# Memory-augmented attention in 64 sequential segments: the order of all engines in a block of four segments written down whole, in place of planned times and rules

## The chip, the cores and the metric

The kernel runs on one core of one Trainium2 chip, in one launch. The metric is the device time of that core in microseconds (us), the median of several runs. TensorE is called PE, VectorE DVE, ScalarE ACT, GpSimd POOL and SyncE SP, as in the profile.

## The reference

Phase 1 is attention over 64 segments of 32 tokens, in which each segment also sees 8 rows of memory: the first 8 output rows of the segment before. Phase 2 is a layer norm and a two-layer MLP. The sequence has 2048 tokens, width 512, 32 heads of 128 (`Wq`, `Wk`, `Wv`: 512 x 32 x 128), and 1792 hidden units.

```python
mem = mem0
for s in range(n_seg):                                   # 64, one after the other
    xs = x[:, s * seg_len:(s + 1) * seg_len, :].copy()
    h = jnp.concatenate([mem, xs], axis=1)               # 8 + 32 rows
    q = jnp.einsum('btd,dhe->bhte', h, Wq)
    k = jnp.einsum('btd,dhe->bhte', h, Wk)
    v = jnp.einsum('btd,dhe->bhte', h, Wv)
    scores = jnp.einsum('bhqe,bhke->bhqk', q, k) * scale
    scores = jnp.where(mask[None, None], scores, -1000000000.0)
    p = _softmax(scores, axis=-1)
    o = jnp.einsum('bhqk,bhke->bhqe', p, v)
    o = jnp.einsum('bhte,hed->btd', o, Wo)
    mem = o[:, :M, :].copy()                             # the next segment needs it
    outs.append(o[:, M:, :])
...
h = x + _A_ref(_layernorm(x, axis=-1), ...)
h2 = h + _B_ref(_layernorm(h, axis=-1), ...)             # layer norm, W1, gelu, W2
```

## The kernel before, in words

All weights lie in SBUF. A segment can't start its projections until the memory rows of the one before are there, so the segments form one long chain, and PE is kept busy in its waits with work that doesn't hang on the memory. Four segments make a block of 128 tokens; a segment's place in its block, its number modulo 4, is called its kind (0 to 3; `sg` in the code).

A segment, in the order of PE, with the names of the tiles:

1. Q and K projections of the 24 + 8 rows that depend on this segment (`hT`; the 8 are the memory rows, put there last by the two additions `hT<-TT`): Q0, Q1, K0, K1, 16 groups of four matmuls with 512 columns, each four in 32-column tiles. `passes` (L858) issues them; L873 is a matmul with its weight load, L606 one that keeps the weights that are there. ACT copies a bank to `kq`, DVE transposes it (`KALL` for K, `QT` for Q; L914), POOL copies Q into `ZC`, which holds it in block form.
2. The scores of the memory rows' queries, in two halves of 16 heads: SC0 and SC1 (`sc_mm`, L1042, `quad<-KALL,ZC`). Between and behind them lie V0 and V1 (`ps<-WV,hT`), the V projections. SC1 needs the transposed K1.
3. Softmax of each half (`sc_softmax`): DVE takes the row maximum of two parts (`nmc`, L1050), ACT the exponentials of each part (`EC`), DVE a reciprocal for each part (`rsc`, L1064) and the scaled product for each part (`PC`, L1067), then one transpose (`PTC`, L1069). The names of the plan are nmc0, ra0, PCa0, rsc0, PC0, PTC0 for the first half (the "a" ones are the first part), and the same with 1 for the second.
4. PV0 and PV1 (`pv_c`, L1080 and L1085): probabilities times V, in 64-row tiles. Between them lie PVA (L1148), the other rows' output of the segment before from the block-diagonal `BD`, and the first WO matmuls. ACT or DVE copies the outputs to `OT` (OTm0, OTm1 for the memory rows, OTx0, OTx1 for the others), the last half of V to `VS` (VS0, VS1, VSl1).
5. WO (L1176, 64 matmuls), its result transposed by DVE (`TT`, L1188), and the two additions to `hT` (L1182), with which the next segment starts. The other rows' additions go to `opT` (opA in the plan).
6. SA (`sa_mm`, L1110): the scores of the other rows, whose softmax runs into the next segment: `nma`, `SA`, `sma`, `rsa` on DVE and ACT, then `PA` on POOL (L1131), `PTA` on DVE (L1133), and four copies `BD` on POOL (L1137).

What doesn't depend on the memory is called F: K, Q and V of the rows that a whole block shares (`hB`, in kinds 0, 1 and 2) and WO for the block before (kind 3), eight groups a segment, spread between the steps above to fill the waits. Its result is folded by seven POOL operations for each half (L1228 to L1232: `TTS`, `TTB`, `opT`), in the segments behind. The layer norm of a later block (`xr`, `agg`, `rst`, `xn`, then copies to `hB` and `hT`) and the residual and statistics of an earlier one are placed there too.

The order on each engine is set by a list scheduler in the kernel (`Sched.schedule`, L237). `ORDERS` gives PE's order for each kind outright. For the other engines each operation has a duration, a fixed hop to its users (`HOP`), and, where `PLAN` has its name, a planned time in the segment; the scheduler takes operations by those times and puts each in the earliest free place of its engine, or of the cheaper of two. For the work that is not in the plan (folds, layer norm, copies of `hB`) rules hand it out behind given operations (`held`, `late`, `now`, `turned`, `fold`, in `tail`).

```python
PLAN = {"kq2": (1.72,) * 4,                              # L43
...
        "rsc0": (5.1,) * 4,
...
        "nmc1": (5.19,) * 4,
...
        "BD": (15.41,) * 4,
...
STEP = 10.28                                             # L102
```

So nearly every name has one time for all four kinds, counted from the segment's first matmul; 10.28 is the step of the plan, the length of a segment in it. `align` (L478) counts PE's instructions and puts up to 8 extra weight loads ("pads") ahead of matmuls, so that a segment of each kind starts at a set place in a fetch block of 256 instructions (`PHASE` (0, 64, 128, 192)).

Of the kernel before, what the change touches and what calls it, by code (L numbers as in the profile page):

```python
# [1694 lines left out]
```

## Time and profile before

| what | us |
|---|---|
| median of 3 runs | 806.22 (805.17, 806.22, 806.32) |
| span of the profiled execution | 804.0 |
| opening: weights arrive, segment 0 | 0 to 51.96 |
| segments 1 to 62 | 51.96 to 689.49: 637.5, 10.28 each |
| segment 63 and phase 2 | 689.49 to 804.0 |

The span of the profile is 2.2 us shorter than the median of the runs; the profile has one time of its own, its span. Times in the text below are microseconds from the span's start, or, where it says "into the segment", from the segment's first Q or K matmul. A row of a timeline has its start, its length, engine, line, operation, tiles (out<-in), shapes, and in brackets the idle time of the engine before it with what ended it.

### The profile page before, as it was taken

What the parts mean: (1) busy time and instruction counts of PE and PEld (TensorE: products, weight loads), DVE (VectorE), ACT (ScalarE), POOL (GpSimd) and SP (SyncE); (2) the same over time, 40 slices, a digit from 0 to 9 for tenths busy, and PEclk for the clock granted to TensorE, in tenths of its full rate; (3) what the DMA queues carried; (4) which work ended last, traced back from release to release, by engine and by line L of the source; (5) the groups of instructions that cost most, each with busy time, mean ns of one, the idle gap of its engine ahead of it and who ended that gap; (6) DMA issues with size and microseconds to landing.
All of it is one profiled execution on the core that took longest, in us unless ns stands there. A gap on an engine that the chain in (4) does not pass through costs nothing.

```text
span 804.0 us, 43669 instructions
## 1 busy us (share of the span) xinstructions
PE 772.7 (96%) x19317; PEld 419.3 (52%) x18821; DVE 616.6 (77%) x1975; ACT 543.0 (68%) x1618; POOL 350.7 (44%) x886
## 2 busy tenths in 40 slices
PE   3788999999999999999999999999999999999998
PEld 1345555555555555555555555555555555544443
DVE  3267898898989898998989898989898887824211
ACT  2456777777777777777777787777777777743342
POOL 5023334545454545454545454545463535367200
PEclk9999999999999999999999999999999999999999
DMA  9960010110101010101010102020212131264200
GB/s 338 393 188 16 4 30 11 27 34 23 37 18 42 18 43 14 46 10 47 8 50 10 49 11 51 10 51 3 51 29 63 37 87 32 89 167 132 69 27 26
DMA packets 65450, 48.04 MB, mean 60 GB/s; under 512 B 29028, under 2 KB 61676, under 8 KB 65260
## 3 DMA queue, kind: packets, MB, share of 16 engines
q1 hardware_dynamic: 64928, 44.98, 18.9%
q8 instruction: 150, 2.46, 1.3%
q14 instruction: 40, 0.33, 0.1%
q10 hardware_dynamic: 332, 0.27, 0.1%
HBM read 31.08 MB, written 8.13 MB: 49 GB/s over the span
## 4 chain that ended last, share of the span: by engine, by line
PE 91%; DVE 3%; DMA 2%; SPq 2%; ACT 1%; issue 0%
PE ps L873 43%; PE ps L1176 16%; PE ps L606 7%; PE quad L1584 6%; PE ps L1577 5%; PE ps L1215 4%; PE quad L1080 3%; DMA WQ<-in_A_Wq_dram 2%; SPq L776 2%; PE ps L1110 2%; PE quad L1042 2%; PE ps L1370 2%; PE quad L1148 1%; PE quad L1085 1%; DVE PC L1067 1%; ACT kq L891 1%
## 5 line engine op out<-in xcount | busy, mean ns | idle before, releaser
L873 PE MATMUL ps<-WQ,hT 128*32 128x512 bf16 x2048 | 157.0, 382 | 3.5 <-DVE hT L1182 3.3
L1176 PE MATMUL ps<-WO,OT 128*32 128x256 bf16 x4224 | 141.5, 275 | 1.0 <-ACT OT L891 1.0
L873 PE MATMUL ps<-WV,hT 128*32 128x512 bf16 x1780 | 138.1, 379 | 0.0
L892 ACT ACTIVATE kq<-ps 128x512 bf16<-128x512 f32 x146 | 87.2, 597 | 57.5 <-PE ps L873 57.2
L1131 POOL TENSOR_TENSOR PA<-SA,rsa 128x256 bf16<-128x256 f32 x64 | 39.8, 622 | 181.4 <-DVE rsa L1124 169.6
L891 ACT CAST kq<-ps 128x512 bf16<-128x512 f32 x160 | 93.3, 583 | 29.8 <-PE ps L873 29.8
L1176 PEld LDWEIGHTS ps<-WO,OT 128*32 128x32 bf16 x4224 | 96.2, 96 | 23.6 <-ACT OT L891 4.0
L1137 POOL COPY BD<-PTA 32x192 bf16<-32x192 bf16 x256 | 95.7, 374 | 16.5 <-DVE PTA L1133 0.8
L1067 DVE SCALAR_TENSOR_TENSOR PC<-EC,rsc,even 128x128 bf16<-128x128 f32 x256 | 94.5, 370 | 6.7
L873 PE MATMUL ps<-WK,hT 128*32 128x512 bf16 x1292 | 92.3, 379 | 0.0
L873 PEld LDWEIGHTS ps<-WQ,hT 128*32 128x32 bf16 x2048 | 56.4, 96 | 63.7 <-issue 19.3
L914 DVE STREAM_TRANSPOSE KALL<-kq 128x256 f32<-128x256 f32 x160 | 70.5, 441 | 21.3 <-ACT kq L891 19.0
L891 ACT CAST VS<-ps 128x512 bf16<-128x512 f32 x189 | 83.9, 444 | 0.9
L1059 ACT ACTIVATE EC<-quad,nmc 128x64 f32<-128x64 f32 x252 | 76.8, 310 | 5.7
L606 PE MATMUL ps<-WK,hT 128*32 128x512 bf16 x756 | 74.3, 379 | 0.0
L891 ACT CAST OT<-quad 128x128 bf16<-128x128 f32 (+1 forms) x208 | 68.4, 352 | 4.9 <-PE quad L1085 0.7
L914 DVE STREAM_TRANSPOSE QT<-kq 128x256 f32<-128x256 f32 x128 | 57.0, 446 | 16.1 <-ACT kq L892 15.0
L873 PEld LDWEIGHTS ps<-WV,hT 128*32 128x32 bf16 x1780 | 49.4, 96 | 34.9 <-issue 1.0
L1580 ACT ACTIVATE WQ<-ps,b1t 128x512 bf16<-128x512 f32 x42 | 28.9, 687 | 52.0 <-PE ps L1577 52.0
L1122 ACT ACTIVATE SA<-SA 128x256 f32<-128x256 f32 x64 | 26.7, 417 | 52.2 <-DVE SA L1121 48.8
L873 PEld LDWEIGHTS ps<-WK,hT 128*32 128x32 bf16 x1292 | 35.9, 97 | 46.6 <-issue 20.2
L1228 POOL TENSOR_TENSOR opT<-TTB,TTS 32x64 bf16<-32x64 f32 x128 | 40.3, 315 | 31.7 <-DVE opT L1182 22.5
(159 smaller groups left out, 1475.9 us busy)
## 6 DMA issues: line engine op xcount, KB each, us to landing
WV<-in_A_Wv_dram SPq DMA_DIRECT2D x4, 1024.0 KB, 10.4
WK<-in_A_Wk_dram SPq DMA_DIRECT2D x4, 1024.0 KB, 18.1
WQ<-in_A_Wq_dram SPq DMA_DIRECT2D x4, 1024.0 KB, 19.4
WO<-in_A_Wo_dram SPq DMA_DIRECT2D x16, 256.0 KB, 7.7
v_last<-VSB SPq DMA_DIRECT2D x60, 64.0 KB, 3.1
VBD<-v_last SPq DMA_DIRECT2D x60, 64.0 KB, 2.9
h_mid<-xr SPq DMA_DIRECT2D x16, 128.0 KB, 1.8
WQ<-h_mid SPq DMA_DIRECT2D x4, 512.0 KB, 4.4
```

The lines of the kernel that those rows point to most:

```text
L606: return e.add_instruction(mybir.InstMatmult(name="I-%d" % (4000000 + _kept[0]), engine=mybir.EngineType.PE, start_tensor_calc=start, stop ...
L873: ins = e.matmul(o, l, m, start=(k == 0), stop=(k == DC - 1), tile_position=(0, 32 * j), skip_group_check=True)
L891: return {"act": (lambda e: e.copy(out, src), t_act(n, ps_)), "dve": (lambda e: e.tensor_copy(out, src), 0.155 + 1.0e-3 * n * fast)}
L892: return {"act": (lambda e: e.mul(out, src, scale_), t_act(n, ps_)), "dve": (lambda e: e.tensor_scalar(out, src, scale_, None, ALU.mult), ...
L914: S.op("dve", lambda e: e.transpose(out, src), reads=[("kq", i)], writes=[key], dur=t_dve(256) + 0.02)
L1059: return e.activation(EC[:, r, sl, :], o[:, sl, :], ACTF.Exp, bias=nmc[:, r, sl:sl + 1], accum_out=smc[:, r, sl:sl + 1])
L1067: S.op("dve", lambda e, sl=sl, xc=xc: e.scalar_tensor_tensor(PC[:, r, :, :, sl], xc, rsc[:, r, sl:sl + 1], ev, ALU.mult, ALU.mult), reads= ...
L1137: S.narrow(S.op("pool", lambda e, j=j, rows=rows: e.tensor_copy(BD[rows, par, :, j, :, :], PTA[rows, :, 0:NA, :]), reads=["PTA"], writes=[ ...
L1176: ins = e.matmul(ps[bank][32 * j:32 * j + 32, 0:256], lhs(slot(h)), wo_cols(h, b), start=(k == 0), stop=(k == 15), tile_position=(0, 32 * ...
L1228: return e.tensor_tensor(o[32 * q:32 * q + 32, c:c + 2], x, y, ALU.add)
L1577: ins = e.matmul(ps[bank][:, 0:SBT], W1[:, cc, fc * P:(fc + 1) * P], hnT_of(k)[:, cc, :], start=(cc == 0), stop=(cc == DC - 1))
L1584: S.op("pe", lambda e: e.matmul(quad[:, t, :], gT_of(k, fc)[:, t * P:(t + 1) * P], W2[:, fc, :], start=(fc == 0), stop=(fc == FC - 1)), re ...
```

## The change

The plan has a time for each operation in each of the four segments of a block, now also for the folds (f0a to f13), the layer norm (lnst, ag, rs, xn, hB, hTx), the residual (xadd, st2a and so on) and each of the four BD copies. These times are no longer wishes: all planned operations of an engine are sorted by them and chained, one after the other, so the order on an engine is the table's. The engine of each operation is in a table of its own (`HOME`, by name and kind), its duration too (`DUR`). The step of the table is 10.181. The rules for folds and the rest are gone.

```diff
-PLAN = {"kq2": (1.72,) * 4,
...
-        "rsc0": (5.1,) * 4,
...
-        "nmc1": (5.19,) * 4,
...
-STEP = 10.28
...
+PLAN = {'kq2': (1.735, 1.758, 1.443, 1.553),
...
+        'rsc0': (5.374, 5.143, 5.398, 5.014),
...
+        'nmc1': (5.16, 5.218, 5.184, 5.194),
...
+        ('ZCm0', 2): 'act',
...
+        ('PCa0', 3): 'pool',
...
+        ('OTx0', 3): 'dve',
+        ('OTx1', 3): 'dve',
...
+STEP = 10.181
+PHASE = 32
...
+        rows = {e: [] for e in ENGINES}
+        for o in self.rec:
+            at = planned(o)
+            if at is not None and not o.is_dma:
+                o.eng = HOME.get((o.kind, o.tag[0] % 4), o.eng)
+                if o.alts:
+                    o.fn, o.dur = o.alts[o.eng]
+                o.dur = DUR.get((o.kind, o.eng), o.dur)
+                rows[o.eng].append((STEP * o.tag[0] + at, o.gidx, o))
+        for row in rows.values():
+            row.sort()
+            for a, b in zip(row, row[1:]):
+                b[2].order = a[2]
+                a[2].succ.append(b[2])
...
-                    t = max(t, q.start + q.dur + (SWITCH if q.mode != o.mode else 0.0))
+                    t = max(t, q.start + q.dur + (SWITCH if q.mode != o.mode and (o.tag is None or o.tag[0] == 0) else 0.0))
...
-            if PHASE and o.tag is not None and o.tag[0] != seg:
-                seg = o.tag[0]
-                owed = (LATE.get(seg, PHASE[seg % 4]) - at) % FETCH_N
+            if o.tag is not None and o.tag[0] // 4 > seg:
+                seg = o.tag[0] // 4
+                owed = (PHASE - at) % FETCH_N
...
+                def halves(e, sl=sl):
+                    return [e.tensor_scalar(PC[:, r, b, :, sl], EC[:, r, sl, :], rsc[:, r, sl:sl + 1], even[:, b:b + 1], ALU.mult, ALU.mult) for b in range(2)][1]
+                S.either({"dve": (whole, 0.37), "pool": (halves, 0.85)}, reads=[ek, rk, "even"], writes=[pk])
...
-            after = [S.last_writer.get(("hTm", (s + 1) % RING))] if s + 1 < NS else []
```

Smaller parts: two operations of one engine that only read the same PSUM bank no longer wait for each other; the pads come once a block; `PA` no longer waits for the next segment's `hT`; hops and durations of some PE operations differ in the planner; the PE orders (`ORDERS`) are new for all kinds. A split of K1 in two (`k_split`) is in the code and used nowhere.

What this does to the streams, at three places. The lines of the changed kernel are other lines of the same operations (L1288 is SC, L1105 and L843 are the projections, L1332 is PV, L1296 nmc, L1311 rsc, L1316 PC, L1321 PTC, L1146 the transposes of `kq`, L1384 PTA).

PE in a segment of kind 0, from SC0 to PV0, before:

```order
L1042 MATMUL quad<-KALL,ZC 32x64 x16
L873 MATMUL ps<-WV,hT 32x512 x4
L606 MATMUL ps<-WV,hT 32x512 x4
L873 MATMUL ps<-WV,hT 32x512 x12
L873 MATMUL ps<-WK,hB 32x512 x4
L1042 MATMUL quad<-KALL,ZC 32x64 x16
L873 MATMUL ps<-WV,hT 32x512 x4
L873 MATMUL ps<-WK,hB 32x512 x4
L873 MATMUL ps<-WV,hT 32x512 x8
L873 MATMUL ps<-WK,hB 32x512 x4
L1080 MATMUL quad<-PTC,VS 128x2x16 x8
```

and now:

```order
L1288 MATMUL quad<-KALL,ZC 32x64 x16
L1105 MATMUL ps<-WV,hT 32x512 x16
L843 MATMUL ps<-WV,hT 32x512 x4
L1288 MATMUL quad<-KALL,ZC 32x64 x16
L1105 MATMUL ps<-WV,hT 32x512 x8
L1105 MATMUL ps<-WK,hB 32x512 x8
L1105 MATMUL ps<-WV,hT 32x512 x4
L1105 MATMUL ps<-WK,hB 32x512 x4
L1332 MATMUL quad<-PTC,VS 128x2x16 x8
```

The second SC, SC1, stood behind six groups after SC0 and now stands behind five; five groups lay between it and PV0, now six. The other three kinds show the same shift, with Q or V of the shared rows, or the last block's WO, in place of `WK,hB`. In kind 1 the last eight matmuls before PV0 are `WV,hT`.

DVE in a segment of kind 0, the softmax of both halves, before:

```order
L1064 RECIPROCAL rsc<-smc 128x1
L1067 SCALAR_TENSOR_TENSOR PC<-EC,rsc,even 128x128
L1064 RECIPROCAL rsc<-smc 128x1
L1050 TENSOR_REDUCE nmc<-quad 128x2
L1067 SCALAR_TENSOR_TENSOR PC<-EC,rsc,even 128x128
L1069 STREAM_TRANSPOSE PTC<-PC 128x128
L1064 RECIPROCAL rsc<-smc 128x1
L1067 SCALAR_TENSOR_TENSOR PC<-EC,rsc,even 128x128
L1064 RECIPROCAL rsc<-smc 128x1
L1067 SCALAR_TENSOR_TENSOR PC<-EC,rsc,even 128x128
L1069 STREAM_TRANSPOSE PTC<-PC 128x128
```

and now:

```order
L1311 RECIPROCAL rsc<-smc 128x1
L1316 SCALAR_TENSOR_TENSOR PC<-EC,rsc,even 128x128
L1296 TENSOR_REDUCE nmc<-quad 128x2
L1311 RECIPROCAL rsc<-smc 128x1
L1316 SCALAR_TENSOR_TENSOR PC<-EC,rsc,even 128x128
L1321 STREAM_TRANSPOSE PTC<-PC 128x128
L1311 RECIPROCAL rsc<-smc 128x1 x2
L1316 SCALAR_TENSOR_TENSOR PC<-EC,rsc,even 128x128 x2
L1321 STREAM_TRANSPOSE PTC<-PC 128x128
```

The row maximum of SC1 (`nmc`) has moved ahead of the first half's second reciprocal (rsc0), in kinds 0 and 2; in kinds 1 and 3 it stays behind it. In kind 3 one `PC` of the first half goes to POOL.

DVE from the transpose of K0 to that of K1, in a segment of kind 1, before:

```order
L914 STREAM_TRANSPOSE KALL<-kq 128x256
L1133 STREAM_TRANSPOSE PTA<-PA 128x128
L914 STREAM_TRANSPOSE QT<-kq 128x256
L1050 TENSOR_REDUCE nmc<-quad 128x2
L914 STREAM_TRANSPOSE KALL<-kq 128x256
```

and now:

```order
L1146 STREAM_TRANSPOSE KALL<-kq 128x256
L1146 STREAM_TRANSPOSE QT<-kq 128x256
L1296 TENSOR_REDUCE nmc<-quad 128x2
L1384 STREAM_TRANSPOSE PTA<-PA 128x128
L1146 STREAM_TRANSPOSE KALL<-kq 128x256
```

`PTA`, which needs POOL's `PA`, stood ahead of the last QT and nmc, and now stands right ahead of the transpose for which SC1 waits; so it is in kind 2 also. On POOL, `PA` now comes behind the first `ZC` copy in kind 1 and behind the copy of `hT` in kind 2.

More of the change, by code (lines that the diff above doesn't have):

```diff
@@ L29 @@
 PAUSES, PAUSE_IN, PAUSE_US = 3, 64, 0.5
-HALVES = ("kq", "KA", "QT", "ZCm", "VS", "VSl", "nmc", "Ea", "EC", "ra", "rsc", "PCa", "PC", "PTC", "OTm", "OTx", "KB", "QTB", "VSB")
+HALVES = ("kq", "KA", "QT", "ZCm", "VS", "VSl", "nmc", "Ea", "EC", "ra", "rsc", "PCa", "PC", "PTC", "OTm", "OTx", "KB", "QTB", "VSB", "opB")
 BONUS = {}
@@ L163, in op @@
                 deps.add(w)
+                if not (excl and w in self.lookers.get(k, ())):
+                    hard.add(w)
             if excl:
@@ L252, in schedule @@
             topo.append(o)
-            for d in o.deps + ([o.prev] if o.prev is not None else []):
+            for d in o.deps + [p for p in (o.prev, o.order) if p is not None]:
                 left[d] -= 1
@@ L299, in schedule @@
             for d in o.deps:
-                t = max(t, d.start + d.dur + self.lat(d, o))
+                t = max(t, d.start + (0.0 if d.eng == o.eng and d in o.soft else d.dur + self.lat(d, o)))
+            if o.order is not None:
+                t = max(t, o.order.start + o.order.dur - OVERLAP[o.eng])
             if o.eng in ("sp", "act") and o.prev is not None:
@@ L578, with directions @@
 MC, MR, MF, MH = 1, 2, 3, 4
-def directions():
+def directions(order):
     back, last = {}, None
-    if not KEEP:
-        return {n: False for n, _, _ in ORDER}
-    for n, lo, hi in ORDER:
-        pack = "A" if n[0] in "KQV" else "B" if n[0] == "F" else None
-        if n[:2] in ("PV", "SC", "SA", "WO"):
-            pack = None
+    for n, lo, hi, was in order:
+        pack = ("A", was) if n in ("K0", "K1", "Q0", "Q1", "V0", "V1") else "B" if n[0] == "F" else None
+        for u in range(lo, hi if pack else lo):
+            if u == 0:
+                back[n] = last == (pack, DC - 1)
+            last = pack, DC - 1 - u % DC if back.get(n, False) != (u >= DC) else u % DC
         if pack is None:
             last = None
-            continue
-        if n not in back:
-            back[n] = last is not None and last == (pack, DC - 1)
-        end = min(hi, DC) - 1
-        last = (pack, DC - 1 - end if back[n] else end)
     return back
@@ L799, in qbf @@
             return quad[:].bitcast(BF16)[:, :, 2 * c0:2 * c0 + P]
-        turned, held, late, now = [], [], [], []
+        held = []
         def ln1(tb, after=()):
@@ L1218, in wo_B @@
                 S.op("pe", f, reads=[("WO", g, a) for g in range(8) for a in range(2)] + [("OTB", bk % 2, sg) for sg in range(4)], writes=[("ps", bank)], dur=0.2135, mode=MC, ni=8)
-            S.op("dve", lambda e: e.transpose(TTB[:].rearrange("p c q t -> p (c q t)"), ps[bank][:, :]), reads=[("ps", bank)], writes=["TTB"], dur=t_dve(512) + 0.02)
+            S.op("dve", lambda e: e.transpose(TTB[:].rearrange("p c q t -> p (c q t)"), ps[bank][:, :]), reads=[("ps", bank)], writes=[("TTB", c) for c in range(2)], dur=0.706, kind="TTB")
@@ L1393, in build_kernel @@
         ln1(0)
-        back = directions()
+        backs = [directions(order) for order in ORDERS]
         for s in range(NS):
             bk, sg = s // 4, s % 4
+            back = backs[sg]
             if s > 0:
@@ L1407, in build_kernel, with take @@
                 {"hx": hx_early, "hn": hn_early, "w1": w1_early}[what](i, here)
+            def take(s, n, lo, hi, was):
+                s += was
+                bk, sg = s // 4, s % 4
+                if s == 0 or s == NS:
+                    return
+                if bk == NTB - 1 and n == "F0":
+                    S.take((s, n), 0, 4 if hi >= 4 else 0)
+                else:
+                    S.take((s, n), lo, None if n[:2] == "SC" else hi)
             def part_F2():
```

566 lines of the change are left out of this document (378 added, 188 removed), and 9 rows, old and new, of tables (EMIT, ORDERS).

## The prediction, made before the changed kernel was run

> **What bounds the kernel now.** I read the share of each engine first, then the chain that ended last, and the busy time of one block of four segments (kinds 0 to 3) beside the sum of twelve blocks (start and end, then length, and busy time of PE, PEld, DVE, ACT, POOL and SP, granted clock, two DMA columns).
>
> ```profile
> PE 772.7 (96%) x19317; PEld 419.3 (52%) x18821; DVE 616.6 (77%) x1975; ACT 543.0 (68%) x1618; POOL 350.7 (44%) x886
> PE 91%; DVE 3%; DMA 2%; SPq 2%; ACT 1%; issue 0%
> 268.52:309.60 41.08, 41.08 (x1173) 22.86 (x1112) 36.98 (x122) 31.10 (x98) 20.34 (x52) 1.00 0.12 30
> ...
> sum 493.51, PE 493.27 PEld 275.08 DVE 442.47 ACT 373.02 POOL 243.30; mean PE 41.11 PEld 22.92 DVE 36.87 ACT 31.08 POOL 20.27
> ```
>
> TensorE is the bound nearly everywhere: 96% busy, 91% of the chain, clock 1.00. Twelve blocks take 493.51 us, 41.13 each, or 10.28 a segment. But "busy" hides short waits, since pipelined matmuls overlap in the records; so I went through one segment matmul by matmul. Segment 28 (first of its block) starts at 329.19, the next at 339.42: 10.23.
>
> ```profile
> 329.19 0.40 PE L873 MATMUL ps<-WQ,hT 128*32 128x512 bf16 x4
> ...
> 334.08 0.29 PE L1042 MATMUL quad<-KALL,ZC 128*32 128x64 bf16 x16
> 334.19 0.39 PE L873 MATMUL ps<-WV,hT 128*32 128x512 bf16 x4
> ...
> 335.06 0.39 PE L873 MATMUL ps<-WK,hB 128*32 128x512 bf16 x4
> 335.41 0.27 PE L1080 MATMUL quad<-PTC,VS 64*128 64x32 bf16 x8
> ...
> 336.11 0.62 PE L1176 MATMUL ps<-WO,OT 128*32 128x256 bf16 x16
> 336.67 0.27 PE L1080 MATMUL quad<-PTC,VS 64*128 64x32 bf16 x8
> 336.93 1.49 PE L1176 MATMUL ps<-WO,OT 128*32 128x256 bf16 x48
> 338.25 0.39 PE L873 MATMUL ps<-WK,hB 128*32 128x512 bf16 x4
> ...
> 339.42 0.40 PE L873 MATMUL ps<-WQ,hT 128*32 128x512 bf16 x4
> ```
>
> Read starts, not lengths. SC1, the second score product (L1042), starts 4.89 into the segment; PV0 (L1080) at 6.22, PV1 at 7.48; the next segment 4.01 after PV0. A group of four 512-column matmuls costs 0.217 (four from 334.19 to 335.06, 0.87). The last group before PV0 is fed by 335.28, PV0 comes at 335.41: PE stood about 0.13 there. PV0 waits for softmax on VectorE, which in turn waited for SC1:
>
> ```profile
> 334.32 0.15 DVE L1064 RECIPROCAL rsc<-smc 128x1 f32<-128x1 f32 x1
> 334.44 0.29 DVE L1050 TENSOR_REDUCE nmc<-quad 128x2 f32<-128x128 f32 x1
> 334.65 0.36 DVE L1067 SCALAR_TENSOR_TENSOR PC<-EC,rsc,even 128x128 bf16<-128x128 f32 x1
> 335.04 0.31 DVE L1069 STREAM_TRANSPOSE PTC<-PC 128x128 f32<-128x128 f32 x1
> ```
>
> **SC1 one group earlier (all four segments).** The new PE order puts SC1 after 21 groups instead of 22. No group goes away; six instead of five now stand between SC1 and PV0. SC1 needs KALL, the transposed last K half. Segment 2, before any memory work of a former block fills the stream, already has SC1 after 21 groups, and shows what that costs (it starts at 62.12):
>
> ```profile
> 62.12 0.41 PE L873 MATMUL ps<-WQ,hT 128*32 128x512 bf16 x4 [0.77 <-DVE hT L1182]
> 66.14 0.82 PE L873 MATMUL ps<-WV,hT 128*32 128x512 bf16 x12
> 66.93 0.30 PE L1042 MATMUL quad<-KALL,ZC 128*32 128x64 bf16 x16
> ...
> 66.43 0.45 DVE L914 STREAM_TRANSPOSE KALL<-kq 128x256 f32<-128x256 f32 x1 [0.17 <-ACT kq L891]
> ...
> 67.32 0.27 DVE L1050 TENSOR_REDUCE nmc<-quad 128x2 f32<-128x128 f32 x1
> ```
>
> KALL (started 4.31 into the segment, as it is 4.30 into segment 29, a row of which stands below) ends at 66.88, SC1 starts 0.05 later, 4.81 into the segment, though its groups were fed at 66.14 + 3 x 0.217 = 66.79. So SC1 can't come before 4.81: 0.08 sooner than in segment 28, where a group less (0.217) was hoped for, and PE stands 0.14 there. The same 16 Q and K groups stay ahead of it, so I take 4.81 for all. Then PV0 by PE: 4.81 + 0.11 (SC1, 334.08 to 334.19) + 6 x 0.217 = 6.22, plus the change from 128-row to 64-row tiles. Its price shows where PV1 waits for nothing but PE, in segment 26:
>
> ```profile
> 315.48 0.61 PE L1176 MATMUL ps<-WO,OT 128*32 128x256 bf16 x16
> 316.03 0.27 PE L1080 MATMUL quad<-PTC,VS 64*128 64x32 bf16 x8
> ```
>
> Sixteen WO matmuls to PV1: 0.55, while 48 of them take 1.32 (336.93 to 338.25), so 16 take 0.44; 0.11 is the change of tiles. Bounds for PV0: 0 and 0.11; I take 0.10, near PV1's case, since the six groups run into PV0 without a gap as WO runs into PV1. PV0 is then at 6.32, 0.10 later than now, in kinds 1 and 3. The Trainium skill's "TensorEngine Tiling (Array Packing)", section Key Properties, says that a change of the tiling mode drains TensorE; by that rule the price falls due at PV0 as well and the sum stands, while at the lower bound, which the rows alone leave open, it would be 805.9. Segment 26's 0.11 agrees with the rule.
>
> **nmc before rsc (kinds 0 and 2).** VectorE now takes SC1's row maximum before the reciprocal of the first half, where both PC and PTC of the first half follow. From the rows above: SC1 to nmc 0.36 to 0.39, take 0.37, so nmc at 5.18; 0.21 from nmc to the next on the queue (334.44 to 334.65), rsc at 5.39; its 0.15 and 0.03 pass, PC at 5.57; 0.39 to PTC, 5.96; 0.37 from PTC to PV0 (335.04 to 335.41): 6.33. It hides behind PE's 6.32, which is why I charge 0.11 here and not their sum. In segments 2, 60 and 62, with fewer groups, nothing covers it: PV0 there goes from 6.14 (row below, 68.26 - 62.12) to 6.33; after it PV1 recovers a part, so 0.13 each, 0.4 in all.
>
> ```profile
> 68.26 0.27 PE L1080 MATMUL quad<-PTC,VS 64*128 64x32 bf16 x8 [0.38 <-DVE rsc L1064]
> ```
>
> **After PV0.** PTC of the second half comes 0.10 earlier relative to PV0, so PV1 is bound by PE: 0.02 saved a segment (PV0 to WO 0.70, WO to PV1 0.55: 1.25, against up to 1.27 now). Behind WO stand four groups and SA (the memory's score product) in every kind, as before: the next segment still waits for WO, TT and hT, so no slack there takes up a late PV0.
>
> **What leaves VectorE's and ScalarE's way.** POOL copies and mask copies move:
>
> ```profile
> 349.20 0.48 DVE L1182 TENSOR_TENSOR hT<-TT 64x32 bf16<-64x32 f32 x2
> 349.04 0.39 POOL L1230 COPY TTS<-TTB 64x256 f32<-64x256 f32 x1
> ...
> 338.96 0.39 DVE L1182 TENSOR_TENSOR hT<-TT 64x32 bf16<-64x32 f32 x2
> ...
> 326.66 0.79 DVE L1182 TENSOR_TENSOR opT<-TT 64x96 bf16<-64x96 f32 x2
> 326.80 0.53 POOL L831 COPY hT<-xT 128x384 bf16<-128x384 bf16 x1
> 326.51 1.56 PE L1176 MATMUL ps<-WO,OT 128*32 128x256 bf16 x48
> ...
> 335.79 0.27 ACT L891 CAST OT<-quad 128x128 bf16<-128x128 f32 x1
> ```
>
> Kind 1 saves the 0.09 by which hT is stretched beside POOL's copy (0.48 against 0.39); there V's last half now ends last before PV0 and its copy on ScalarE may hold up the first OT cast, which comes 0.38 behind PV0 (335.79 in segment 28); between 0 and the 0.09 that would eat the gain, I take 0.02: -0.07. In kind 3 OT's second half is no longer behind mask copies, and WO's 48 take 1.32 instead of 1.39 (1.56 against 1.49 with the same tail): -0.07; and opT (0.79) no longer runs beside POOL's hT copy; it makes TT late by 0.14 in four of fourteen blocks, so -0.04. The Trainium skill's "SBUF — State Buffer", section "SBUF: two separate sides", calls the port pair that VectorE and GpSimd share an exclusive lock whose loser blocks for the whole instruction. By that rule hT would have stood until the copy ended at 349.43, 0.23 instead of 0.09, the term would be -0.21 and the sum 806.4; the trace shows less, and the trace's 0.09 is taken.
>
> **Pads and the rest.** Pads (extra weight loads that shift the fetch phase) now stand only in kind 0. The first group of segment 29, which has none, takes 0.22 (339.42 to the first row here), that of segment 30, which has some, 0.23:
>
> ```profile
> 339.64 0.40 PE L606 MATMUL ps<-WK,hT 128*32 128x512 bf16 x4
> ...
> 349.75 0.40 PE L873 MATMUL ps<-WQ,hT 128*32 128x512 bf16 x4
> 349.98 0.39 PE L606 MATMUL ps<-WK,hT 128*32 128x512 bf16 x4
> ```
>
> So kinds 2 and 3 save 0.01, and kind 1, which has none today, already does. The 22 pads of kind 0 lie between matmuls, beside a weight-load path that is busy 52%: bounds 0 and 22 x 0.01 a block, taken as 0. The opening and phase 2 keep their work and order: 0.
>
> **Sum.** A block: PV0 later by 0.11, 0.09, 0.10 and 0.09 (kinds 0 to 3), +0.39; PV1, 4 x -0.02; kind 1, -0.07; kind 3, -0.11; together +0.13 on the 41.13 of now. Fourteen blocks (segments 4 to 59): +1.8. Segments 2, 60 and 62: +0.4. The profiled execution goes from 804.0 to 806.2; the 2.2 between its span and the median of the runs (806.22) stay outside. **808.4 us**, +0.27%. A fifth of a per cent, 1.6 us, is about what can be told here from no change.
>
> **Rivals.**
> - *The earlier SC1 pays.* If softmax and PE both gain, PV0 comes in all kinds where segment 2 has it, 6.14 instead of 6.22: 4 x 0.08, with PV1 and the gains of kinds 1 and 3 0.58 a block, some 798. The kernel's own table steps 10.181 a segment after 10.28 before, which is 6 less, 800. Against it: segment 2 has few groups between SC1 and PV0; and the planner's rules drop the 0.1 for a change of tiles, where segment 26 shows 0.11.
> - *The change of tiles hides at PV0.* Then kinds 1 and 3 stay at 6.22 while kinds 0 and 2 go to 6.33 by VectorE: 0.18 a block less than forecast, -0.05: 805.9, no change.
> - *Everything at PV0 hides.* If KALL and SC1 come early enough that PV0 stays in all kinds, the gains of kinds 1 and 3 and PV1's are left: -0.26 a block, 802.6.
> - *POOL is late (slower).* In kinds 1 and 2 the transpose PTA now stands on VectorE between nmc and KALL's last transpose, and waits for POOL's PA. Today PTA stands a transpose further ahead, and PA ends at 342.11, 0.5 before it:
>
> ```profile
> L1228 POOL TENSOR_TENSOR opT<-TTB,TTS 32x64 bf16<-32x64 f32 x128 | 40.3, 315 | 31.7 <-DVE opT L1182 22.5
> ...
> 341.49 0.62 POOL L1131 TENSOR_TENSOR PA<-SA,rsa 128x256 bf16<-128x256 f32 x1 [1.60 <-DVE rsa L1124]
> 342.64 0.27 DVE L1133 STREAM_TRANSPOSE PTA<-PA 128x128 f32<-128x128 f32 x1
> 343.72 0.45 DVE L914 STREAM_TRANSPOSE KALL<-kq 128x256 f32<-128x256 f32 x1 [0.17 <-ACT kq L891]
> ```
>
> The new order puts PA behind ZCm (kind 1) and behind hT's copy (kind 2). VectorE idles 0.17 ahead of KALL; PTA takes 0.27. From a PA that ends later than about 4.0 into the segment, each 0.1 makes SC1, PV0 and the segment 0.1 longer. At 0.1 in two kinds of each block: +2.8, 811. In kind 3 a PC moves to POOL as two instructions, each between 0.315 (a 32x64 sum) and 0.622 (PA's 128x256); its 128x64 halves are nearer the first, so it ends by 5.6 and is covered by nmc and the other PC.
>
> **Chances.** Forecast 0.40 (0.30 of it above 807.8, 0.10 below); the change of tiles hides 0.20; the earlier SC1 pays 0.10; everything hides 0.10; POOL late 0.20. Faster 0.20, same 0.30, slower 0.50. The range leaves out the case near 800 and the worse half of POOL: 802.5 to 811.
>
> **What would show it.** Right: SC1 at 4.80 to 4.82 in every segment behind KALL, with PE idle ahead of it; PV0 at 6.31 to 6.34; nmc ahead of rsc in kinds 0 and 2; hT 0.39 in all kinds. Wrong: PV0 at 6.22 or earlier, SC1 behind POOL's PA, PC of kind 3 over 0.9 on POOL, or PE waiting at PVA for BD.

## The result: 1.7% slower, and the profile after

The changed kernel takes 819.19 us (median of 4 runs, 816.61 to 821.5) beside 805.69 for the kernel before on the same chip: ratio 1.0167, 95% interval 1.015 to 1.0185. Forecast were 808.4, in a range of 802.5 to 811. The profiled span went from 804.0 to 818.8.

From the page after: share of each engine, and the chain that ended last. Then the busy time of one block (kinds 0 to 3, segments 28 to 31) and the sum of twelve, in the columns of before.

```profile
PE 782.5 (96%) x19317; PEld 398.5 (49%) x18445; DVE 583.0 (71%) x1910; ACT 549.0 (67%) x1683; POOL 350.6 (43%) x902
...
PE 78%; DVE 11%; ACT 5%; DMA 3%; SPq 2%; issue 1%; POOL 0%; DVEq 0%
...
334.25:376.06 41.81, 41.68 (x1176) 21.67 (x1123) 34.38 (x118) 31.47 (x101) 20.31 (x53) 1.00 0.12 31
...
sum 502.06, PE 500.38 PEld 260.51 DVE 411.60 ACT 377.64 POOL 241.28; mean PE 41.70 PEld 21.71 DVE 34.30 ACT 31.47 POOL 20.11
```

PE looks as busy as before, 96%, but its part of the chain fell from 91% to 78%, and VectorE's rose from 3% to 11%, although VectorE has 34 us less to do: PE now waits for VectorE. The granted clock is 1.00 in the block. Start of a segment to start of the next, mean of the 14 segments of a kind (segments 4 to 59), and PV0's median start in it, in us:

| | before: length | PV0 | after: length | PV0 |
|---|---|---|---|---|
| kind 0 | 10.242 | 6.211 | 10.470 | 6.478 |
| kind 1 | 10.329 | 6.229 | 10.340 | 6.340 |
| kind 2 | 10.227 | 6.209 | 10.569 | 6.454 |
| kind 3 | 10.327 | 6.217 | 10.443 | 6.407 |
| segments 60, 61, 62 | 10.45, 10.33, 10.38 | | 13.60, 10.98, 10.71 | |

The kinds add up to 41.125 and 41.822: 0.70 a block, 9.8 us in 14 blocks. Segments 60 to 62 add 4.1, segments 1 to 3 0.5, opening and phase 2 0.4: 14.8, the whole difference of the spans. In each kind PV0 comes later (0.81 a block); from PV0 on, the block as a whole gains 0.11, though kind 2 loses there too.

TensorE in segment 28 (kind 0), SC1, PV0, PV1 and the next segment:

```profile
334.25 0.41 PE L1105 MATMUL ps<-WQ,hT 128*32 128x512 bf16 x4
...
339.06 0.30 PE L1288 MATMUL quad<-KALL,ZC 128*32 128x64 bf16 x16
...
340.73 0.27 PE L1332 MATMUL quad<-PTC,VS 64*128 64x32 bf16 x8
...
341.98 0.26 PE L1332 MATMUL quad<-PTC,VS 64*128 64x32 bf16 x8
...
344.71 0.40 PE L1105 MATMUL ps<-WK,hT 128*32 128x512 bf16 x4
```

SC1 is at 4.81, as forecast, but PV0 is at 6.48 where 6.33 was forecast. VectorE and POOL ahead of it, after, and then POOL's copy at that place before:

```profile
339.43 0.29 DVE L1296 TENSOR_REDUCE nmc<-quad 128x2 f32<-128x128 f32 x1
339.63 0.15 DVE L1311 RECIPROCAL rsc<-smc 128x1 f32<-128x1 f32 x1
339.82 0.51 DVE L1316 SCALAR_TENSOR_TENSOR PC<-EC,rsc,even 128x128 bf16<-128x128 f32 x1
340.36 0.31 DVE L1321 STREAM_TRANSPOSE PTC<-PC 128x128 f32<-128x128 f32 x1
339.83 0.34 POOL L1388 COPY BD<-PTA 32x192 bf16<-32x192 bf16 x1
```

```profile
334.72 0.48 POOL L1137 COPY BD<-PTA 32x192 bf16<-32x192 bf16 x1
```

PC took 0.51 instead of 0.36, and ends 0.16 behind POOL's copy, which took its usual 0.34. Before, PC had started at 334.65, 0.07 ahead of the copy; there PC took 0.36, and the copy 0.48, and it ended 0.19 behind PC. So the two don't run together: one goes first, and the other finishes a fixed time behind it. Which one goes first hangs on the starts, and where they nearly meet it is POOL's copy: here PC began 0.01 ahead of it and was still held. In segments 4 to 58 of the two traces this holds row by row: 151 PCs that began with or behind a copy or a sum of POOL, of which 0.21 to 0.39 was still to run, ended 0.16 behind its end (0.155 to 0.168); 93 PCs that met one with 0.17 or less to run kept 0.35 to 0.37; 69 BD copies that began 0.04 to 0.2 behind a PC ended 0.19 behind that PC (0.188 to 0.200); 153 PCs with no POOL work beside them took 0.35 to 0.38. Before, the PC that met a BD copy like this began only 0.04 to 0.08 ahead of it: the margin was small, and in kinds 0 and 2 the change used it up. The Trainium skill's "SBUF — State Buffer", section "Who interferes with whom", says that a VectorE instruction with two SBUF inputs contends with a GpSimd instruction that reads SBUF, that the shared port pair is an exclusive lock, and that the order of issue decides who blocks; the rows agree, but for the few hundredths between starts at which POOL's copy, begun later, goes first. They add the price: behind the copy PC still needs 0.16, less than its own 0.36.

Kind 2 (segment 30, from 355.06) has the same, PC 0.01 behind a BD copy; behind PV0 it loses again: the two PCs of the second half meet POOL's copies as well (0.89 for both; PV1 comes 1.32 behind PV0, 1.26 before), and `hT` now stands behind `agg`, so that it starts 0.54 behind TT and not 0.49 (kind 2 after, and then before):

```profile
360.62 0.34 POOL L1388 COPY BD<-PTA 32x192 bf16<-32x192 bf16 x1
360.63 0.48 DVE L1316 SCALAR_TENSOR_TENSOR PC<-EC,rsc,even 128x128 bf16<-128x128 f32 x1
...
361.54 0.89 DVE L1316 SCALAR_TENSOR_TENSOR PC<-EC,rsc,even 128x128 bf16<-128x128 f32 x2
...
364.64 0.45 DVE L1439 STREAM_TRANSPOSE TT<-ps 128x256 f32<-128x256 f32 x1 [1.29 <-PE ps L1427]
365.02 0.14 DVE L1045 BATCH_NORM_AGGREGATE agg<-stt 128x2 f32<-128x6 f32 x1
365.18 0.39 DVE L1433 TENSOR_TENSOR hT<-TT 64x32 bf16<-64x32 f32 x2
```

```profile
369.30 0.45 DVE L1188 STREAM_TRANSPOSE TT<-ps 128x256 f32<-128x256 f32 x1
369.79 0.39 DVE L1182 TENSOR_TENSOR hT<-TT 64x32 bf16<-64x32 f32 x2
```

Kind 3 (segment 31, from 365.63) waits for the PC that went to POOL:

```profile
370.64 0.91 POOL L1319 TENSOR_SCALAR PC<-EC,rsc,even 128x64 bf16<-128x64 f32 x2 [0.21 <-ACT EC L1305]
371.66 0.31 DVE L1321 STREAM_TRANSPOSE PTC<-PC 128x128 f32<-128x128 f32 x1 [0.30 <-POOL PC L1319]
```

At the end of segment 60 PE waits for a DMA transpose that feeds phase 2. The timeline of PE after, then that of SP's queue after, and of SP's queue before:

```profile
681.38 1.04 PE L1607 MATMUL ps<-xr,hT 128*128 128x512 bf16 x4 [2.92 <-DMA xr<-xn]
```

```profile
668.94 0.43 SPq L1503 DMA_DIRECT2D h_mid<-xr  x1
...
677.25 1.23 SPq L1595 DMA_TRANSPOSE xr<-xn  x1
```

```profile
646.56 0.33 SPq L1266 DMA_DIRECT2D h_mid<-xr  x1
...
652.55 1.22 SPq L1358 DMA_TRANSPOSE xr<-xn  x1
```

The last transposed rows come 24.7 later, while the segment itself starts only 10.4 later; the store of the last residual rows, which frees a slot of `xr`, comes 22.4 later.

### The profile page after: what moved, and what is told of

It reads as the page before. It is cut to its first block, busy times and chain, and to the rows that moved or that the text cites. A ratio compares the mean times of both kernels' runs of the same rounds, so it can differ in the third digit from the quotient of the medians.

```text
span 818.8 us, 43353 instructions
## 1 busy us (share of the span) xinstructions
PE 782.5 (96%) x19317; PEld 398.5 (49%) x18445; DVE 583.0 (71%) x1910; ACT 549.0 (67%) x1683; POOL 350.6 (43%) x902
## 4 chain that ended last, share of the span: by engine, by line
PE 78%; DVE 11%; ACT 5%; DMA 3%; SPq 2%; issue 1%; POOL 0%; DVEq 0%
PE ps L1105 31%; PE ps L1427 15%; PE ps L843 6%; PE quad L1810 6%; PE ps L1803 4%; DVE PC L1316 4%; PE quad L1332 3%; PE ps L1463 3%; ACT kq L1123 3%; DMA WQ<-in_A_Wq_dram 2%; SPq L1013 2%; PE ps L1362 2%; DVE KALL L1146 2%; PE ps L1607 2%; PE quad L1399 1%; DVE PTC L1321 1%
## 5 line engine op out<-in xcount | busy, mean ns | idle before, releaser
L1105 PE MATMUL ps<-WV,hT 128*32 128x512 bf16 x1844 | 129.8, 379 | 0.0
L1105 PE MATMUL ps<-WQ,hT 128*32 128x512 bf16 x1612 | 126.6, 380 | 2.1 <-DVE hT L1433 2.1
L1105 PE MATMUL ps<-WK,hT 128*32 128x512 bf16 x1484 | 116.4, 379 | 1.0 <-DVE hT L1433 1.0
L1124 ACT ACTIVATE kq<-ps 128x512 bf16<-128x512 f32 x160 | 95.7, 598 | 30.9 <-PE ps L1105 30.6
L1123 ACT CAST OT<-quad 128x128 bf16<-128x128 f32 (+1 forms) x223 | 80.5, 361 | 46.3 <-PE quad L1337 45.8
L1388 POOL COPY BD<-PTA 32x192 bf16<-32x192 bf16 x256 | 89.1, 348 | 23.1 <-DVE PTA L1384 9.1
L1316 DVE SCALAR_TENSOR_TENSOR PC<-EC,rsc,even 128x128 bf16<-128x128 f32 x240 | 93.7, 403 | 5.1
L1146 DVE STREAM_TRANSPOSE KALL<-kq 128x256 f32<-128x256 f32 x160 | 70.1, 438 | 14.5 <-ACT kq L1123 13.1
L1105 PEld LDWEIGHTS ps<-WQ,hT 128*32 128x32 bf16 x1612 | 42.3, 96 | 73.7 <-issue 27.1
L1174 POOL COPY ZC<-QT 128x128 bf16<-128x128 bf16 x110 | 32.0, 291 | 104.4 <-DVE QT L1146 101.5
L1105 PEld LDWEIGHTS ps<-WK,hT 128*32 128x32 bf16 x1484 | 40.4, 97 | 62.7 <-issue 30.3
L1146 DVE STREAM_TRANSPOSE QT<-kq 128x256 f32<-128x256 f32 x128 | 56.9, 444 | 18.6 <-ACT kq L1124 12.2
L1439 DVE STREAM_TRANSPOSE TT<-ps 128x256 f32<-128x256 f32 x66 | 29.2, 442 | 50.1 <-PE ps L1427 50.0
L1105 PEld LDWEIGHTS ps<-WV,hT 128*32 128x32 bf16 x1844 | 42.7, 96 | 27.6 <-issue 1.4
L843 PE MATMUL ps<-WK,hT 128*32 128x512 bf16 x564 | 55.3, 379 | 0.0
```

Source lines behind the costliest of these rows:

```text
L843: return e.add_instruction(mybir.InstMatmult(name="I-%d" % (4000000 + _kept[0]), engine=mybir.EngineType.PE, start_tensor_calc=start, stop ...
L1105: ins = e.matmul(o, l, m, start=(k == 0), stop=(k == DC - 1), tile_position=(0, 32 * j), skip_group_check=True)
L1123: return {"act": (lambda e: e.copy(out, src), t_act(n, ps_)), "dve": (lambda e: e.tensor_copy(out, src), 0.155 + 1.0e-3 * n * fast)}
L1124: return {"act": (lambda e: e.mul(out, src, scale_), t_act(n, ps_)), "dve": (lambda e: e.tensor_scalar(out, src, scale_, None, ALU.mult), ...
L1146: S.op("dve", lambda e: e.transpose(out, src), reads=[("kq", i)], writes=[key] + list(more), dur=t_dve(256) + 0.02)
L1316: return e.scalar_tensor_tensor(PC[:, r, :, :, sl], xc, rsc[:, r, sl:sl + 1], ev, ALU.mult, ALU.mult)
```

## The experiments

Theory A says what the last section reads: PC held by a POOL copy that starts with it or before, PC on POOL in kind 3, and the late `xr` at the end. The rivals stand in the expectations. Lengths are medians of a kind unless they are called means, and come from the one profiled execution of each run; in the changed kernel the medians are 10.457, 10.337, 10.569 and 10.438 (kinds 0 to 3), in the kernel before 10.224, 10.329, 10.218 and 10.292. Ratios are to the kernel before, with 95% intervals.

**e1: rsc0 ahead of nmc again, in kinds 0 and 2**

```diff
-        'rsc0': (5.374, 5.143, 5.398, 5.014),
+        'rsc0': (5.134, 5.143, 5.158, 5.014),
```

> Changed kernel with one edit: in kinds 0 and 2 the first half's reciprocal rsc0 comes ahead of SC1's row maximum nmc again, as it does in kinds 1 and 3. Theory A (port): a VectorE operation with two SBUF inputs (PC) that starts just behind a POOL copy is held until that copy's end + 0.16. PC0 then starts at 5.45 instead of 5.57, between two POOL copies instead of beside the start of one, takes 0.36 instead of 0.48 to 0.51, and PV0 is set by PE at 6.34: kind 0 10.46 to 10.32, kind 2 10.57 to 10.38; 814 in all. Theory B (order alone): PC is long for itself in these kinds; only the 0.12 of the order goes, PC0 stays near 0.5, PV0 6.36 to 6.40, kind 0 10.38, kind 2 10.50; 817.

815.09 us, ratio 1.0118 (1.0092 to 1.0144). Kind 0 takes 10.322, kind 2 10.379, PV0 is at 6.343 and 6.338. Segment 28:

```profile
337.57 0.36 DVE L1316 SCALAR_TENSOR_TENSOR PC<-EC,rsc,even 128x128 bf16<-128x128 f32 x1
337.97 0.31 DVE L1321 STREAM_TRANSPOSE PTC<-PC 128x128 f32<-128x128 f32 x1
337.76 0.36 POOL L1388 COPY BD<-PTA 32x192 bf16<-32x192 bf16 x1
```

PC begins 0.19 ahead of the copy and keeps its 0.36. One reciprocal in another place is worth 4 us in the medians of the runs; in the two profiles kinds 0 and 2 give 4.6, and segments 60 to 62 are 2.3 shorter besides.

**e2: the order of the change, and one more POOL operation ahead of BD in kind 0**

```diff
+        'dum': (5.5, None, None, None),
...
+                if sg == 0:
+                    S.op("pool", lambda e: e.memset(scr[:], 0.0), writes=["scr"], dur=0.12, kind="dum")
```

> Changed kernel with one POOL operation more in each kind 0 (a 128x32 memset that only writes, about 0.12, between the ZC copy and the BD copy that starts beside PC0). Theory A (port, first come): the BD copy starts 0.15 behind PC0's start instead of beside it, so POOL is held and not VectorE: PC0 0.36 instead of 0.51, PV0 6.34 instead of 6.48, kind 0 10.32 instead of 10.46, 817.3 in all, though POOL has more to do. Theory B (PC is long for itself, or POOL's load as such slows it): PC0 stays at 0.5 or more, kind 0 10.46 or longer, 819 to 820.

820.49, ratio 1.0191 (1.0153 to 1.0228). PV0 of kind 0 goes to 6.343, but the segment still takes 10.489.

```profile
341.29 0.12 POOL L1696 MEMSET scr<- 128x32 bf16 x1
341.41 0.37 DVE L1318 SCALAR_TENSOR_TENSOR PC<-EC,rsc,even 128x128 bf16<-128x128 f32 x1
341.47 0.49 POOL L1390 COPY BD<-PTA 32x192 bf16<-32x192 bf16 x1
342.04 0.72 POOL L1478 TENSOR_TENSOR TTB<-TTB,TTS 64x256 f32<-64x256 f32 x1
342.21 0.72 DVE L1318 SCALAR_TENSOR_TENSOR PC<-EC,rsc,even 128x128 bf16<-128x128 f32 x1
```

More work on POOL makes the first PC faster, because the copy now comes 0.06 behind it. That part was foreseen. Missed was what follows: the later copy moves the fold `TTB`, which now begins ahead of the second half's first PC, and that PC takes 0.72. The loss is handed on to PV1.

**e3: the PC of kind 3 on DVE**

```diff
-        ('PCa0', 3): 'pool',
+        ('PCa0', 3): 'dve',
```

> Changed kernel with one edit: in kind 3 the first PC of the first half is back on VectorE (one operation) instead of POOL (two). Theory A: POOL's two take 0.91 (0.42 and 0.53, the second held by VectorE's PC) and end at 5.93, so PTC waits 0.3 for them; on VectorE PV0 is set by PE at 6.34 and kind 3 takes 10.36 instead of 10.44: 818 in all. Theory B (VectorE is too full in kind 3): PV0 stays at 6.40 or later, no gain.

818.03, ratio 1.016 (1.0139 to 1.0181). PV0 of kind 3 goes from 6.407 to 6.341, as expected; the length only to 10.425. So POOL's PC is the 0.07 of kind 3 ahead of PV0, and other things hold the rest: the first PC is now held by a BD copy (0.53), and WO starts later behind the copy OTm0.

**e4: SC1 one group later in all kinds, as before the change**

```diff
-('V0', 0, 4, 0), ('V1', 0, 1, 0), ('SC1', 0, 1, 0), ('V1', 1, 3, 0),
+('V0', 0, 4, 0), ('V1', 0, 2, 0), ('SC1', 0, 1, 0), ('V1', 2, 3, 0),
```

> Changed kernel with PE's order alone changed: SC1 one group of four matmuls later in all kinds, as in the kernel before (five groups between SC1 and PV0 instead of six). Theory A: kind 1 is bound by PE at PV0, so it gains the group that stood behind the wait for KALL, PV0 6.34 to 6.23, 10.34 to 10.23; in kinds 0 and 2 PC0 is asked for 0.07 later but is let go by the same POOL copy at the same time, PV0 6.45 to 6.48 as now; in kind 3 POOL's PC sets PV0 at 6.41 as now: 1.6 less, 817.5. Theory B (the chain of softmax from SC1 sets kinds 0 and 2): +0.07 there, 10.53 and 10.64, in all no change. Theory C (PE's idle ahead of SC1 costs every kind): 0.1 less in all, 813.5.

822.22, ratio 1.0199 (1.0174 to 1.0225). That can't be told from the changed kernel (the intervals overlap); 817.5 was expected. Kinds 0 and 2 stay at 10.457 and 10.566: the time at which SC1 comes changes nothing there, since PC ends with the same POOL copy. Kind 3, expected to stay, falls to 10.377: VectorE's own PC comes later there, and POOL's two halves take 0.80 in place of 0.91. Kind 1 was expected shorter and is longer, 10.418, as its PC now meets a copy (segment 29):

```profile
350.25 0.34 POOL L1388 COPY BD<-PTA 32x192 bf16<-32x192 bf16 x1
350.28 0.47 DVE L1316 SCALAR_TENSOR_TENSOR PC<-EC,rsc,even 128x128 bf16<-128x128 f32 x1
```

**e5: e1, and the copies of `hB` and `hT` for the last blocks out of the table**

```diff
+    if o.kind in ("hB", "hTx") and o.tag[0] > 48:
+        return None
```

> The kernel with rsc0 first in kinds 0 and 2, and one edit more: POOL's last copies out of xT (hB and hTx of the layer norm issued in segment 50) are not held to the table's late places (five segments on), so that the rows for phase 2 that are loaded into xT from segment 54 on are not late. Theory A: segment 60 ends with W1 matmuls that wait for the last of these rows' transposes (2.9 in the changed kernel); with xT free early that wait goes, segment 60 takes 10.3 instead of 12 to 13.6 and the kernel 1.7 to 3 less than with rsc0 alone, 812 to 813. Theory B: the wait comes from phase 2's own loads and stays.

818.08, ratio 1.0142 (1.0116 to 1.0167). Segment 60 takes 15.37, in e1 12.00. The rows for `xT` do load sooner (from 593 us into the span on, in the changed kernel from 622), but the last transpose of `xr` still comes at 673.7. The idea that the copies from `xT` hold it back fell.

**e6: PC on DVE as two operations with one tensor input**

```diff
-                    return e.scalar_tensor_tensor(PC[:, r, :, :, sl], xc, rsc[:, r, sl:sl + 1], ev, ALU.mult, ALU.mult)
+                    return [e.tensor_scalar(PC[:, r, b, :, sl], EC[:, r, sl, :], rsc[:, r, sl:sl + 1], even[:, b:b + 1], ALU.mult, ALU.mult) for b in range(2)][1]
```

> Changed kernel with PC on VectorE as two operations with one SBUF input each (scalars for the rest) instead of one with two inputs. Theory A (the port is shared by VectorE's second input and POOL): no PC is held by a POOL copy any more, its halves take the same time beside a copy and alone (within 0.03) in all kinds, and no BD copy is stretched to 0.47 beside a PC. The time of a half isn't known; at 0.20 each the softmax is no longer than before and PV0 is set by PE at 6.34 in kinds 0 to 2, 813; at 0.30 each the chain of kinds 0 and 2 is 0.1 longer than now, 820. Theory B (POOL slows any VectorE operation): the halves are longer where a POOL copy starts beside them, up to 0.15.

866.47, ratio 1.0754. Segment 28, the two halves of one PC and POOL beside the second:

```profile
360.22 0.33 DVE L1316 TENSOR_SCALAR PC<-EC,rsc,even 128x64 bf16<-128x64 f32 x1
360.45 0.73 DVE L1316 TENSOR_SCALAR PC<-EC,rsc,even 128x64 bf16<-128x64 f32 x1
360.35 0.77 POOL L1476 TENSOR_TENSOR TTB<-TTB,TTS 64x256 f32<-64x256 f32 x1
```

A half takes 0.31 to 0.33 with no POOL work beside it, and 0.73 when it begins 0.10 behind POOL's sum; it ends 0.06 behind that. So one tensor input is no way round the hold, where theory A expected that it would be; as a cure it is worse, since two halves take longer than the whole. The same section of the Trainium skill counts `tensor_scalar` among the operations that can take the shared pair; the rows agree.

**e7: the kernel before, with POOL's fold moved away from `hT` in kind 1**

```diff
-(3, 5, 6, 0)[s % 4]
+(4, 4, 6, 0)[s % 4]
```

> The kernel before with one number changed: four of the fourteen fold operations behind kind 0 and four behind kind 1, instead of three and five. POOL's copy TTS then doesn't run beside hT's additions (two SBUF inputs) at the end of kind 1. Theory A (port): hT's first half takes 0.19 instead of 0.27, kind 1 10.33 to 10.24, thirteen blocks, 1.2 less, 804.5. Theory B (the 0.09 is of another cause): no change.

805.35 against 806.02, ratio 0.9995 (0.9983 to 1.0006). Kind 1 goes from 10.329 to 10.244 and the first `hT` from 0.27 to 0.19, as expected; kind 0 has single longer segments (mean 10.291) that eat part of it, and the rest can't be told from nothing.

**e8: several cures at once**

e1, e3, e4 and e5, small POOL operations that hold the folds back until the last PC is done, folds of kind 3 moved, `agg` behind `hT`.

```diff
-        'ag': (None, None, 9.656, None),
+        'ag': (None, None, 10.17, None),
```

> The changed kernel with all that the runs so far point to: SC1 one group later, rsc0 first in kinds 0 and 2, kind 3's PC on VectorE, xT free early; POOL's folds behind a small operation that waits for the last PC of the segment (kinds 0 to 2), some folds and ZC copies moved so that no POOL copy starts within 0.12 ahead of a PC; the layer norm's statistics behind hT in kind 2. Theory A: PV0 6.21 to 6.24 in all kinds, no PC over 0.39, lengths 10.21 to 10.25, 802.5, faster than the kernel before by 0.4%. Theory B: copies that are late because they were moved (BD, before PVA) take the gain back: PV0 right but PVA or hT late, 10.3, 805 to 808.

818.04, ratio 1.0157 (1.0135 to 1.0179). Kinds 0 and 1 come to 10.233 and 10.241, as expected, kind 2 to 10.313; but kind 3 takes 11.19, as `agg` behind `hT` makes POOL late, and SC0 with it; and segment 60, with the edit of e5, 15.16.

**e9: e8 mended**

`agg` ahead of TT (8.4), OTm0 of kind 3 ahead of VS, the edit of e5 dropped, and the folds of segment 55 within the next two segments, in place of the table's places. Some ZC copies and statistics were moved too.

```diff
+                if sg in (0, 1, 2):
+                    S.op("pool", lambda e: e.memset(scr[:], 0.0), reads=[("PC", 1), ("PCa", 1)], writes=["scr"], dur=0.12, kind="gate")
...
+    if o.tag[0] == 55 and o.kind in ENDS:
+        return ENDS[o.kind]
```

> As the first retuned kernel (SC1 one group later, rsc0 first, kind 3's PC on VectorE, folds behind the last PC), with its kind 3 mended: the layer norm's aggregation on VectorE stands ahead of TT in kind 2, so that POOL's chain in kind 3 (rst, folds, PA, ZC) starts as early as in the changed kernel and SC0 isn't late; OTm0 ahead of VS1 on ScalarE in kind 3; the statistics and the ZC copy of kind 2 moved out of hT's way; the last block's folds (segment 55) placed in the next two segments instead of four; the xT edit left out. Theory A: kinds 0 and 1 10.23 and 10.24 as measured there, kind 2 10.25 instead of 10.31, kind 3 10.25 instead of 11.2, segment 60 10.4: 804 in all, about 0.2% faster than the kernel before. Theory B: without the late kind 3 another wait shows there, 10.3 or more: 806 and no gain.

807.33, ratio 1.0013 (1.0004 to 1.0022). The kinds come to 10.226, 10.234, 10.245 and 10.295, PV0 to 6.24 to 6.27, segments 60 to 62 to 10.51, 10.68 and 10.45. Segment 28, PC ahead of the copy, and PV0 at 6.24:

```profile
334.71 0.36 DVE L1322 SCALAR_TENSOR_TENSOR PC<-EC,rsc,even 128x128 bf16<-128x128 f32 x1
334.81 0.45 POOL L1394 COPY BD<-PTA 32x192 bf16<-32x192 bf16 x1
335.48 0.27 PE L1338 MATMUL quad<-PTC,VS 64*128 64x32 bf16 x8
```

So 12 of the 13.5 us are undone by moving a few operations within the written-out order: POOL's folds and copies, rsc0, the PC of kind 3, `agg`, OTm0, and SC1 put back. Which of them e9 needs wasn't tried. The 804 that was hoped for isn't reached, nor the time of the kernel before.

**e10: the changed kernel, and the folds of segment 55 within the next two segments, alone**

```diff
+ENDS = {"f0a": 17.5, "f0b": 17.9, "f0c": 18.7, "f00": 19.1, ...
+    if o.tag[0] == 55 and o.kind in ENDS:
+        return ENDS[o.kind]
```

> Changed kernel with one edit: POOL's fourteen folds of the block that is issued in segment 55 come in segments 56 and 57 instead of over the table's five segments. Theory A: they end the chain (fold, transposed output, residual, store, a buffer of xr coming free, the transposed rows for W1) on which the W1 matmuls at the end of segment 60 wait; with them earlier that wait (2.9) goes, segment 60 takes 10.4 to 10.5 instead of 13.6, the kernel 3 less, 816. Theory B (phase 2's own loads): segment 60 stays above 12.

817.62, ratio 1.0139 (1.0124 to 1.0155). Segment 60 goes from 13.60 to 10.76, segment 61 from 10.98 to 10.29, the wait for `xr` is gone, and SP issues the last transpose 14 sooner:

```profile
663.09 1.23 SPq L1599 DMA_TRANSPOSE xr<-xn  x1
```

In the nine profiles of the changed order without this edit segment 60 takes 12.0 to 15.4, in the three with it (e9, e10, e11) 10.5 to 10.8. That shows the cause of the loss at the end: the folds of the last block, placed late in the table, hold up the residual rows, their store, and the slot of `xr`. The gain in the median, 1.6, is less than the 3 hoped for and not clear of noise (the intervals overlap); segment 56, into which part of the folds moved, takes 11.02.

**e11 and e12: pads in each segment again, on e9 and on the changed kernel**

```diff
-            if o.tag is not None and o.tag[0] // 4 > seg:
-                seg = o.tag[0] // 4
-                owed = (PHASE - at) % FETCH_N
+            if o.tag is not None and o.tag[0] != seg:
+                seg = o.tag[0]
+                owed = (LATE.get(seg, PHASES[seg % 4]) - at) % FETCH_N
```

> The retuned order (e9) with the pads set in each segment again (phases 0, 64, 128, 192, as in the kernel before) instead of once a block. Theory A (the 0.2 to 0.5 us stalls at weight loads of SA, which stand at no wait that the profile shows, belong to the place in the instruction stream): kind 3 falls from a mean of 10.35 to about 10.29, the single long segments of kinds 0 and 1 (10.78, 10.47) mostly go, 1.4 us in all: 805.9, against 807.3 for e9, no difference from before. Rival B (the stalls have nothing to do with the place): 807.3, kind 3 stays at 10.35 with lengths up to 10.55.

> The changed kernel with nothing but the pads set in each segment again, as before the change. Theory A (PC held by POOL's copy and the late xr transpose make the loss; the pads matter only in single stalls): the medians of the kinds stay at 10.457, 10.337, 10.569 and 10.438, PV0 6.478 in kind 0; only the single stalls go (segments 19, 48 and 61, about 1.0 together): 818.2. Rival B (the pads once a block make the loss): the kinds fall to 10.3 and the time to about 808.

e11: 806.99, ratio 1.0006 (0.9996 to 1.0016), not to be told from e9. Kind 3 has a mean of 10.331 and still single segments of 10.5 to 10.68, and kind 1 is 0.04 longer. e12: 821.79, ratio 1.0196 (1.0176 to 1.0217); kinds 10.490, 10.372, 10.559 and 10.401. So the pads are no part of the loss (rival B of e12 is out), and the 1 us that was hoped for didn't come. What the single stalls hang on (in e9 the row below, idle with nothing that the profile shows as its end) stays open: theory A of e11 isn't borne out either.

```profile
452.77 0.22 PE L1368 MATMUL ps<-KALL,QT 128*32 128x32 bf16 x6 [0.20 <-issue]
```

## Why the prediction was right in sign and wrong in size and cause

- **SC1 one group earlier**: right. SC1 is at 4.81 in all but one of segments 4 to 59, held by KALL, and where PE alone sets PV0 (kind 1; e1 in kinds 0 and 2) it comes at 6.34, forecast 6.32, with the change of tiles in it. With the holds taken away (e1, and e3 for kind 3) PV0 is 0.11 to 0.13 later than before in every kind, forecast 0.09 to 0.11: so far the sign is no luck. The rivals in which the earlier SC1 pays, or the change of tiles hides, are out.
- **nmc before rsc**: the order was right and the price wrong; this is the step that failed inside the blocks. The chain took PC from segment 28 of before, "0.39 to PTC", as a price that PC carries with it. It was the price of a PC that begins 0.07 ahead of POOL's copy. The step puts PC 0.11 later into the segment, to where the copy goes first, and the copy has no term in the chain. PC took 0.51 and 0.48, and PV0 came 0.15 and 0.12 later than the forecast of 6.33. e1 takes this away alone: kinds 0 and 2 then lie at 10.32 and 10.38.
- **The rule set aside**: the lock was named and weighed at `hT` of kind 1, and dropped because "the trace shows less", 0.09. The first of the two additions, taken by itself, shows the hold:

```profile
349.20 0.27 DVE L1182 TENSOR_TENSOR hT<-TT 64x32 bf16<-64x32 f32 x1
```

  It ends at 349.47, 0.05 behind POOL's copy (349.04 + 0.39), as in all 11 such blocks of before (0.046 to 0.050), and took 0.27 where it takes 0.19 alone; with the copy away (e7) it takes 0.19. The prediction let the rule cost 0.23, all that was left of the copy. But a held operation doesn't lengthen by what is left; it ends a fixed time behind. The small 0.09 was what the meeting happened to leave, and was taken for the size of the effect.
- **PC of kind 3 on POOL**: wrong. It was put at an end by 5.6 into the segment and ended at 5.93: its halves take 0.42 and 0.54 (over the 0.9 in all that the prediction named as a sign of being wrong), the second while VectorE's own PC runs, and it starts only at 5.02, when ACT's EC is there. PTC waits 0.30, PV0 comes at 6.41.
- **After PV0**: PV0 to PV1 is 1.25 in kind 0, as forecast; the stretch of `hT` in kind 1 is gone, and kind 1 is 0.10 shorter behind PV0 (forecast 0.09). Kind 2 lost 0.10 there, which was not foreseen: the second half's PCs are held as well (0.44 and 0.55), and `agg` stands ahead of `hT`. Kind 3 gained 0.06 of the forecast 0.13, kind 0 0.05. In all -0.11 (by the means) for the -0.26 of the sum.
- **Segments 60 to 62, and the opening and phase 2**: the second step that failed. The sum gave segments 60 to 62 under 0.3, for PV0 alone, and nothing for a wait at their end; they took 4.1 longer than before. The opening and phase 2, put at 0, took 0.4 longer. The time at which the last folds are done had moved, and behind them stood a DMA transpose. The prediction followed the moved operations within a block and not the last block's out to their last user.
- **POOL late at KALL**: did not come; KALL begins at 4.31. POOL did make much of the loss in kinds 0 and 2, but by holding PC and not by handing over its result late.

Of the 0.81 that PV0 came later in a block, 0.39 was forecast; with -0.11 instead of -0.26 behind PV0 this makes 0.70 instead of 0.13 a block; 9.8 us of blocks, 4.1 of the end, 0.9 of start and phase 2 are the 14.8 between the spans, where 2.2 was forecast. Of the 12.6 that were missed, 4.3 lie ahead of PV0 in kinds 0 and 2 (PC behind POOL's copy), 1.2 ahead of it in kind 3 (PC on POOL), 0.3 in kind 1, 2.1 behind PV0, and 4.6 outside the blocks, 3.9 of them in segments 60 to 62.

## What to carry to other kernels

When an order is moved by a tenth of a microsecond on VectorE, look up what POOL runs in that tenth: two operations that hold each other don't run side by side, they run in an order, and 0.1 us of shift can cost 0.15 a segment or nothing. Price such a meeting by where the other operation ends, not by how much longer the row was last time. When background work moves within a repeated block, follow the last block's copy of it to its last user, since the steady state doesn't show what it holds up at the end.
